# The last 1 MB of an output projection: one row slot sent in 102 + 26 partitions, two more cut by columns, the result stored in three parts

## The chip, the cores and the metric

The kernel runs on one core of a Trainium2 chip. The metric is device time of one execution in microseconds (us): the median of several runs. A profile of one execution gives a span, from the first to the last instruction.

## The reference

Four tokens (B = 4, one position each, D = 1024) pass through a cached attention block and a gated MLP, and the two results are mixed. Cut to what matters:

```
g = sigmoid((x * gate_w).sum(-1))
q = x @ wq                                   # wq: 1024 x 4096, 32 heads of 128
p = softmax(q . k_cache / sqrt(128))         # k_cache, v_cache: 4 x 32 x 8192 x 128, bf16
a = (p . v_cache) @ wo                       # wo: 4096 x 1024
b = x + sigmoid(x.w_r) * ((silu(x @ w_gate) * (x @ w_up)) @ w_down)
out = g * a + (1 - g) * b                    # 4 x 1 x 1024, bf16
```

The caches are 256 MB each, so the program is one long stream of reads from HBM: 576 MB in all, against 8 KB written.

## The kernel before

All large reads go through one SBUF buffer, the `ring`, and are issued by SyncE (SP) in one fixed order. The K pairs and V pairs of the cache come first, alternating; while they stream, VectorE transposes K, TensorE computes scores and the weighted sums, and the gate/up/down weights are read in between. `wo` (8 MB) comes last, as eight blocks `g` of 1 MB. A block holds 512 rows of `wo`: partition `p` gets rows `4p` to `4p+3`, four "row slots" of 1024 columns (2 KB) each (`wov`, `FR = 4`). Blocks 0 and 1, and 2 and 3, come in one transfer each (`wo_two`, L455); blocks 4 to 6 in one transfer each; block 7 is cut: row slots 0 and 1 together (128 partitions x 4 KB), row slot 2 (128 x 2 KB), and row slot 3 in two halves of 512 columns (128 x 1 KB each). These are issued in `wo_block` (L439, L442).

Of each transfer, 16 DMA engines carry a share. SP has eight completion semaphores for its transfers and uses them in turn, so that a transfer is issued only when the one eight places ahead of it has landed.

`wo_block` also returns `use()`, the matmuls of that piece: for each row slot, one matmul of 512 columns into `acc(0)` and one into `acc(1)` (through `mm_acc`, L296), with `LT`, the transposed attention result, as the weights. `acc(0)` and `acc(1)` are two PSUM banks that hold output columns 0 to 511 and 512 to 1023; everything of the output is summed up there. `acc(0)` lies on partitions 0 to 3 and `acc(1)` on 32 to 35, so a pair of matmuls, one into each, runs side by side.

After the last `use()`, VectorE copies `acc(0)` to SBUF as bf16 (L694) and SP stores it (L695); ScalarE copies `acc(1)` (L696) and issues its store itself (L697). SP then waits for the completion of every semaphore, and all engines meet at a barrier (L723).

The order of the engines' instructions is the order in which the program is written (a manual schedule). `keep_weights` drops repeated weight loads, `drop_implied` drops waits that another wait already implies.

Of the kernel before, what the change touches and what calls it, by code (L numbers as in the profile page):

```python
# [112 lines left out]
def kernel(  # L113
# [15 lines left out]
    nc = tc.nc  # L129
    P = 128  # L130
    Bn, Sq, D = A_x.shape
# [17 lines left out]
    FR = 4  # L149
    FG = F // (P * FR)  # L150
    NB = 512
    NH = D // NB
# [7 lines left out]
    out2 = out.rearrange("b s d -> (b s) d")  # L160
# [28 lines left out]
    def turned(rows, n, dtype=BF, lo=0):  # L189
        t = TB[tb_turn[0] % 2]  # L190
        tb_turn[0] += 1
        return t[lo:lo + rows, 0:n] if dtype == BF else t[lo:lo + rows, 0:2 * n].bitcast(dtype)
# [46 lines left out]
    n = 1  # L239
# [19 lines left out]
    for half in range(2):  # L259
        for e in range(2):  # L260
            nc.gpsimd.tensor_copy(out=R[:, 2 * half + e].rearrange("p (n j) -> p n j", n=4),
                                  in_=ident[:, 64 * half + e:64 * half + 64:2].unsqueeze(1).to_broadcast([P, 4, 32]))
# [21 lines left out]
    LT = const.tile([P, FR, H // FR, Bn], BF)  # L284
# [7 lines left out]
    def acc(n):  # L292
        return A_ps[n][32 * n:32 * n + Bn]

    def mm_acc(n, lhsT, rhs, start=False):
        nc.tensor.matmul(acc(n), lhsT=lhsT, rhs=rhs, start=start, stop=True, skip_group_check=True)  # L296
# [36 lines left out]
    wov = A_wo.rearrange("(g p r) n -> p g r n", p=P, r=FR)  # L333
# [86 lines left out]
    NWB = H // WB  # L420
# [8 lines left out]
                                 rhs=OT[:, WB * g0 + k:WB * g1:WB, :], start=True, stop=True, skip_group_check=True)  # L429
        nc.vector.tensor_copy(out=LT[:, :, g0:g1, :], in_=lp)  # L430

    def wo_block(g, r0=0, r1=FR, half=None, load=True):

        at = wo_places[g] * FR * D
        w = flat[:, at:at + FR * D].rearrange("p (r n) -> p r n", r=FR)
        if not load:
            pass
        elif half is None:
            nc.sync.dma_start(out=w[:, r0:r1].rearrange("p r n -> p (r n)"),  # L439
                              in_=wov[:, g, r0:r1].rearrange("p r n -> p (r n)"))  # L440
        else:
            nc.sync.dma_start(out=w[:, r0, half * NB:(half + 1) * NB], in_=wov[:, g, r0, half * NB:(half + 1) * NB])  # L442

        def use():
            for r in range(r0, r1):
                for n in range(NH) if half is None else [half]:
                    mm_acc(n, LT[:, r, g, :], w[:, r, n * NB:(n + 1) * NB])
        return use


    def wo_two(g):

        at = wo_places[g] * FR * D
        assert wo_places[g + 1] == wo_places[g] + 1
        nc.sync.dma_start(out=flat[:, at:at + 2 * FR * D].rearrange("p (g n) -> p g n", g=2),  # L455
                          in_=wov[:, g:g + 2].rearrange("p g r n -> p g (r n)"))
        return [wo_block(g, load=False), wo_block(g + 1, load=False)]
# [14 lines left out]
    def flush_sums():  # L472
        while full:
            full.pop(0)()
# [186 lines left out]
    for kind, d in order:  # L661
# [11 lines left out]
        if (kind, d) == ("v", ND - 1):  # L673
            first, second = wo_two(0)
            first()
            last = [second]
# [2 lines left out]
        if (kind, d) == ("v", ND - 2):  # L679
            o_rows(0, GE)  # L680
    last += wo_two(2)
    cuts = [(g, 0, FR) for g in range(4, NWB - 1)] + [(NWB - 1, 0, 2), (NWB - 1, 2, 3)] + [(NWB - 1, FR - 1, FR, n) for n in range(NH)]
    last += [wo_block(*cut) for cut in cuts]
    flush_sums()
    for _ in range(2):
        last.pop(0)()
# [4 lines left out]
    for use in last:  # L691
        use()
    res = [turned(Bn, NB, lo=32 * n) for n in range(NH)]
    nc.vector.tensor_copy(out=res[0], in_=acc(0))  # L694
    nc.sync.dma_start(out=out2[:, 0:NB], in_=res[0])  # L695
    nc.scalar.copy(out=res[1], in_=acc(1))  # L696
    nc.scalar.dma_start(out=out2[:, NB:D], in_=res[1])  # L697


# [28 lines left out]
```

## Time and profile before

| what | us |
|---|---|
| median of 3 runs | 1341.02 (1340.89 to 1341.03) |
| span of the profiled execution | 1339.17 |
| outside the span, against the median | 1.85 |
| last `wo` transfer landed, from the span's start | 1335.98 |
| last matmul ends | 1336.40 |
| stores landed (SP's, ScalarE's) | 1338.09, 1338.33 |

The page gives the span in 40 slices, the DMA engines' busy share and the bytes per second, the chain of work that ended last, and groups of instructions. The times of landing are records of the trace: each DMA engine that carried a part of a transfer adds one to the transfer's semaphore when its part is written, and each such step has a time. A transfer over all 128 partitions has 16 of them.

### The profile page before, as it was taken

The numbers are of one execution on the slowest core, as the hardware profiler recorded it, in microseconds if no ns is written. First come the engines' busy times: TensorE is split into PE (matmuls) and PEld (weight loads), VectorE is DVE, ScalarE is ACT, GpSimd is POOL, SyncE is SP. The second block draws the span as 40 slices with busy tenths as digits, with TensorE's granted clock in tenths as the row PEclk, the third lists the DMA queues.
The fourth block names the chain that finished last, engine by engine and source line by source line (L and its number), as shares of the span: only waits on it lengthen the run. The fifth ranks groups of instructions, "written<-read, shape, count | busy, mean of one in ns | idle before, by whom it ended". The sixth has DMA issues, their size and how long they took to land.

```text
span 1339.2 us, 6936 instructions
## 1 busy us (share of the span) xinstructions
PE 1031.3 (77%) x4654; PEld 139.8 (10%) x1486; DVE 638.7 (48%) x385; ACT 57.7 (4%) x58; POOL 67.0 (5%) x174
## 2 busy tenths in 40 slices
PE   2386787887777788777787977777797778687887
PEld 0011000001010010101001110100111011111111
DVE  2285998556553436555352556634345556100001
ACT  0000000100010000100010000100000000110000
POOL 2000000100010000100010000100001000100000
PEclk9697998898888998888889988888998889689999
DMA  9999999999999999999999999999999999999998
GB/s 415 433 437 437 435 437 435 420 438 433 433 435 437 427 433 435 429 438 431 433 431 433 435 439 427 429 433 435 438 430 428 433 429 429 438 429 445 422 422 352
DMA packets 13032, 576.14 MB, mean 430 GB/s; under 512 B 1436, under 2 KB 1700, under 8 KB 1970
## 3 DMA queue, kind: packets, MB, share of 16 engines
q1 hardware_dynamic: 12994, 575.69, 99.6%
q8 instruction: 24, 0.39, 0.1%
q14 instruction: 6, 0.05, 0.0%
q10 hardware_dynamic: 8, 0.00, 0.0%
HBM read 575.68 MB, written 0.01 MB: 430 GB/s over the span
## 4 chain that ended last, share of the span: by engine, by line
DMA 67%; PE 22%; DVE 9%; POOL 0%; ACT 0%; issue 0%; SPq 0%
DMA ring<-in_A_k_cache_dram 53%; PE S_ps L516 15%; DMA ring<-in_A_v_cache_dram 10%; DVE ring L511 9%; PE o_ps L587 5%; DMA ring<-in_B_w_gate_dram 3%; DMA ring<-in_A_wo_dram 2%; PE o_ps L342 1%; POOL PB L570 0%; DVE mx L536 0%; PE led L633 0%; ACT TB L545 0%; PE acc L296 0%; POOL Z L492 0%; PE o_ps L633 0%
## 5 line engine op out<-in xcount | busy, mean ns | idle before, releaser
L511 DVE STREAM_TRANSPOSE ring<-ring 128x2048 uint32<-128x2048 uint32 x256 | 566.5, 2276 | 307.7 <-DMA ring<-in_A_k_cache_dram 307.7
L516 PE MATMUL S_ps<-ring,Z 128*128 128x512 bf16 x2048 | 519.9, 408 | 229.3 <-DVE ring L511 216.1
L587 PE MATMUL o_ps<-ring,PB 128*64 128x512 bf16 x2048 | 457.4, 384 | 35.7 <-DMA ring<-in_A_v_cache_dram 33.3
L516 PEld LDWEIGHTS <-Z 128*128 128x128 bf16 x512 | 53.0, 104 | 683.0 <-issue 683.0
L617 DVE SCALAR_TENSOR_TENSOR OS<-o_ps,mE,OS 128x512 f32<-128x512 f32 x33 | 24.8, 751 | 161.7 <-ACT OS L613 160.2
L587 PEld LDWEIGHTS <-PB 128*64 128x64 bf16 x512 | 56.7, 111 | 428.3 <-issue 427.6
L625 DVE SCALAR_TENSOR_TENSOR OS<-o_ps,mE,OS 128x512 f32<-128x512 f32 x5 | 3.7, 750 | 143.6 <-ACT OS L623 143.6
L492 POOL COPY Z<-qa 32x4 bf16<-32x4 bf16 x128 | 25.8, 201 | 716.7 <-PE S_ps L516 689.6
L570 POOL COPY PB<-PT 32x1024 bf16<-32x1024 bf16 (+3 forms) x23 | 33.4, 1452 | 466.6 <-PE o_ps L587 360.7
L613 ACT ACTIVATE OS<-o_ps,mE 128x512 f32<-128x512 f32 x11 | 7.6, 687 | 671.2 <-PE o_ps L587 671.2
L568 ACT COPY PB<-PT 32x1024 bf16<-32x1024 bf16 (+3 forms) x21 | 30.3, 1444 | 22.4 <-PE o_ps L587 17.4
L545 ACT ACTIVATE TB<-S_ps,mx 128x2048 bf16<-128x2048 f32 x4 | 7.9, 1967 | 321.7 <-DVE mx L542 321.7
L254 PE MATMUL S_ps<-identb,x 6*128 6x6 bf16 x8 | 0.6, 196 | 22.3 <-DMA x<-in_gate_w_dram 22.3
L342 PE MATMUL o_ps<-ring,xw 128*4 128x512 bf16 (+2 forms) x128 | 12.9, 490 | 3.5 <-DMA ring<-in_B_w_gate_dram 3.5
L633 PEld LDWEIGHTS o_ps<-selg,OS 128*128 128x128 f32 x88 | 11.5, 191 | 8.8 <-issue 8.5
L550 DVE STREAM_TRANSPOSE PT<-TB 128x2048 bf16<-128x2048 bf16 x4 | 9.2, 2312 | 6.4 <-ACT TB L545 6.4
L296 PE MATMUL acc<-ring,hT 128*4 128x512 bf16 x54 | 7.9, 466 | 5.5 <-DMA ring<-in_B_w_down_dram 5.5
L536 DVE TENSOR_REDUCE mx<-S_ps 128x1 f32<-128x2048 f32 x4 | 9.1, 2282 | 6.0 <-PE S_ps L516 6.0
L296 PE MATMUL acc<-ring,LT 128*4 128x512 bf16 x64 | 8.8, 378 | 3.3 <-DMA ring<-in_A_wo_dram 2.8
L633 PE MATMUL o_ps<-selg,OS 128*128 128x8 f32 x88 | 10.5, 245 | 0.0
L623 ACT ACTIVATE OS<-o_ps,mE 128x512 f32<-128x512 f32 x5 | 3.4, 687 | 151.2 <-PE o_ps L587 151.2
L256 DVE COPY xw<-S_ps 128x48 bf16<-128x48 bf16 x1 | 0.2, 184 | 17.5 <-PE S_ps L254 17.5
(83 smaller groups left out, 88.4 us busy)
## 6 DMA issues: line engine op xcount, KB each, us to landing
ring<-in_A_v_cache_dram SPq DMA_DIRECT2D x7, 4096.0 KB
ring<-in_A_k_cache_dram SPq DMA_DIRECT2D x6, 4096.0 KB, 33.9
ring<-in_A_v_cache_dram SPq DMA_DIRECT2D x6, 2048.0 KB, 28.9
ring<-in_B_w_gate_dram SPq DMA_DIRECT2D x1, 7168.0 KB
ring<-in_B_w_up_dram SPq DMA_DIRECT2D x1, 7168.0 KB
ring<-in_B_w_down_dram SPq DMA_DIRECT2D x1, 6912.0 KB
ring<-in_A_wo_dram SPq DMA_DIRECT2D x2, 2048.0 KB
ring<-in_A_wo_dram SPq DMA_DIRECT2D x3, 1024.0 KB, 34.5
```

What stands on the lines that cost most here:

```text
L296: nc.tensor.matmul(acc(n), lhsT=lhsT, rhs=rhs, start=start, stop=True, skip_group_check=True)
L342: nc.tensor.matmul(ps[32 * k:32 * k + Bn, z, :].rearrange("p (f r) -> p f r", r=FR)[:, :, lo:hi], lhsT=xT[TW * half + t], rhs=rhs, start=( ...
L492: nc.gpsimd.tensor_copy(out=Z[at, :, QP - 1 + QP * q], in_=qa[at, :, h0 + q, b])
L511: nc.vector.transpose(out=kn[:, half], in_=kn[:, half])
L516: nc.tensor.matmul(sps[:, z, :], lhsT=Z[:, 2 * half + e, s:s + P], rhs=T[:, half, 16 * z:16 * z + 16, :, e], start=(t + k + half + e == 0) ...
L536: nc.vector.tensor_reduce(out=mx[:, 0:1], in_=sps[:].rearrange("p z n -> p (z n)"), axis=AX.X, op=ALU.max)
L550: nc.vector.transpose(out=PT[:].rearrange("p j i -> p (j i)"), in_=PTs)
L568: nc.scalar.copy(out=Bv[at, :, :, q, :], in_=Pv[at])
L570: nc.gpsimd.tensor_copy(out=Bv[at, :, :, q, :], in_=Pv[at])
L587: nc.tensor.matmul(o_ps[w // 2][row:row + NM, w % 2, :], lhsT=PB[:, RD * (d % NW) + n, z].rearrange("p w s j -> p (w s j)"), rhs=vn[:, j0 ...
L617: nc.vector.scalar_tensor_tensor(out=OS[:], in0=o_ps[w // 2][:, w % 2, :], scalar=mE[:, w:w + 1], in1=OS[:], op0=ALU.mult, op1=ALU.add)
L633: nc.tensor.matmul(oT, lhsT=OS[:, q * Dh:(q + 1) * Dh], rhs=selg[:, q].rearrange("p t s -> p (t s)"), start=(q == 0), stop=(q == 3), skip_ ...
```

## The change

In the last block, row slots 0 and 1 are no longer one transfer. Row slot 0 is a transfer of its own (128 x 2 KB). Row slot 1 is sent as two transfers, partitions 0 to 101 and 102 to 127. Row slots 2 and 3 are cut by columns: columns 0 to 767 of both slots in one transfer (128 x 2 x 1.5 KB), then columns 768 to 1023 of slot 2 and of slot 3 in one transfer each (128 x 0.5 KB). The bytes are the same; four transfers become six. `use()` follows the cuts: columns 512 to 767 and 768 to 1023 become separate matmuls of 256 columns.

At the end, ScalarE now copies and stores `acc(0)`; VectorE copies `acc(1)` in two parts of 256 columns, and SP stores each part. The other blocks go through the same rewritten `wo_block` with the same transfers as before.

```diff
-    def wo_block(g, r0=0, r1=FR, half=None, load=True):
+    def wo_block(g, r0=0, r1=FR, cols=(0, D), load=True, spans=((0, P),)):
 
         at = wo_places[g] * FR * D
+        c0, c1 = cols
         w = flat[:, at:at + FR * D].rearrange("p (r n) -> p r n", r=FR)
-        if not load:
-            pass
-        elif half is None:
-            nc.sync.dma_start(out=w[:, r0:r1].rearrange("p r n -> p (r n)"),
-                              in_=wov[:, g, r0:r1].rearrange("p r n -> p (r n)"))
-        else:
-            nc.sync.dma_start(out=w[:, r0, half * NB:(half + 1) * NB], in_=wov[:, g, r0, half * NB:(half + 1) * NB])
+        for p0, p1 in spans if load else ():
+            if c1 - c0 == D:
+                nc.sync.dma_start(out=w[p0:p1, r0:r1].rearrange("p r n -> p (r n)"),
+                                  in_=wov[p0:p1, g, r0:r1].rearrange("p r n -> p (r n)"))
+            else:
+                nc.sync.dma_start(out=w[p0:p1, r0:r1, c0:c1], in_=wov[p0:p1, g, r0:r1, c0:c1])
 
         def use():
             for r in range(r0, r1):
-                for n in range(NH) if half is None else [half]:
-                    mm_acc(n, LT[:, r, g, :], w[:, r, n * NB:(n + 1) * NB])
+                for n in range(NH):
+                    lo, hi = max(c0, n * NB), min(c1, (n + 1) * NB)
+                    if lo < hi:
+                        nc.tensor.matmul(acc(n)[:, lo - n * NB:hi - n * NB], lhsT=LT[:, r, g, :], rhs=w[:, r, lo:hi],
+                                         start=False, stop=True, skip_group_check=True)
         return use
...
-    cuts = [(g, 0, FR) for g in range(4, NWB - 1)] + [(NWB - 1, 0, 2), (NWB - 1, 2, 3)] + [(NWB - 1, FR - 1, FR, n) for n in range(NH)]
-    last += [wo_block(*cut) for cut in cuts]
+    LC = D - NB // 2
+    cuts = [(g, 0, FR) for g in range(4, NWB - 1)] + [(NWB - 1, 0, 1), (NWB - 1, 1, 2), (NWB - 1, 2, FR, (0, LC))]
+    cuts += [(NWB - 1, r, r + 1, (LC, D)) for r in range(2, FR)]
+    last += [wo_block(*cut, spans=((0, 102), (102, P)) if cut[1:3] == (1, 2) and cut[0] == NWB - 1 else ((0, P),)) for cut in cuts]
...
     res = [turned(Bn, NB, lo=32 * n) for n in range(NH)]
-    nc.vector.tensor_copy(out=res[0], in_=acc(0))
-    nc.sync.dma_start(out=out2[:, 0:NB], in_=res[0])
-    nc.scalar.copy(out=res[1], in_=acc(1))
-    nc.scalar.dma_start(out=out2[:, NB:D], in_=res[1])
+    nc.scalar.copy(out=res[0], in_=acc(0))
+    nc.scalar.dma_start(out=out2[:, 0:NB], in_=res[0])
+    for lo, hi in ((0, LC - NB), (LC - NB, NB)):
+        nc.vector.tensor_copy(out=res[1][:, lo:hi], in_=acc(1)[:, lo:hi])
+        nc.sync.dma_start(out=out2[:, NB + lo:NB + hi], in_=res[1][:, lo:hi])
```

## The prediction

> **What bounds the kernel now.** First the page: span, bytes per second by slice, and the chain that ended last.
>
> ```profile
> span 1339.2 us, 6936 instructions
> ...
> GB/s 415 433 437 437 435 437 435 420 438 433 433 435 437 427 433 435 429 438 431 433 431 433 435 439 427 429 433 435 438 430 428 433 429 429 438 429 445 422 422 352
> ...
> q8 instruction: 24, 0.39, 0.1%
> ...
> DMA 67%; PE 22%; DVE 9%; POOL 0%; ACT 0%; issue 0%; SPq 0%
> ```
>
> The stream runs at 415 to 445 GB/s until the last slice, 352. The change touches the last megabyte of 576, so all it can reach lies in that slice. Next the chain in order of time and the timeline, both at the end:
>
> ```profile
> 1311.27 24.05 DMA ring<-in_A_wo_dram
> 1335.32 0.04 issue
> 1335.36 1.05 PE acc L296 x4
> 1336.41 0.02 issue
> 1336.43 0.58 ACT TB L696
> ```
>
> ```profile
> 1334.70 1.69 PE L296 MATMUL acc<-ring,LT 128*4 128x512 bf16 x8 [0.22 <-DMA ring<-in_A_wo_dram]
> 1336.12 0.68 DVE L694 CAST TB<-acc 4x512 bf16<-4x512 f32 x1 [6.49 <-PE acc L296]
> 1336.43 0.58 ACT L696 CAST TB<-acc 4x512 bf16<-4x512 f32 x1 [10.90 <-PE acc L296]
> 1336.83 0.29 SPq L695 DMA_DIRECT2D out_dram<-TB  x1
> 1337.04 0.55 ACTq L697 DMA_DIRECT2D out_dram<-TB  x1
> ```
>
> The end hangs on the last `wo` landing, then one matmul, one copy, one store, the barrier. Last, the DMA share in windows (the last two columns are DMA share and GB/s):
>
> ```profile
> 1328.00:1330.00 2.00, 2.00 (x35) 1.09 (x35) 0.43 (x2) 0.00 (x0) 0.00 (x0) 1.00 1.02 422
> 1330.00:1332.00 2.00, 1.22 (x10) 0.35 (x8) 0.00 (x0) 0.00 (x0) 0.00 (x0) 1.00 0.91 362
> 1332.00:1333.00 1.00, 0.02 (x2) 0.00 (x0) 0.00 (x0) 0.00 (x0) 0.00 (x0) 1.00 0.65 264
> 1333.00:1334.00 1.00, 0.54 (x6) 0.26 (x7) 0.00 (x0) 0.00 (x0) 0.00 (x0) 1.00 0.74 276
> 1334.00:1335.00 1.00, 0.78 (x10) 0.25 (x5) 0.00 (x0) 0.00 (x0) 0.00 (x0) 1.00 0.54 201
> ```
>
> From 1330 on the share falls: some DMA engines are out of work while others go on. The landing records of the last `wo` transfer say how many (us after 1331.23, one number per engine):
>
> ```
> 0.00 0.22 0.32 0.69 | 2.97 2.97 3.21 3.53 | 4.34 4.37 4.44 4.48 4.51 4.54 4.66 4.75
> ```
>
> Four engines are early, four in the middle, eight late. Perfect balance would end at the mean, 3.13, a gain of 1.6 us, or 0.12%. About 0.2% (2.7 us) is what a measurement of this kernel can tell from no change, so this step is small by construction.
>
> **Which engine is which.** The landings count the engines a transfer uses: 16 for 128 partitions, 8 for the 8-row transfer of `w_down`, 4 for the 4 rows of `x`, and 3 for its 12-row transfers, whose source is 3 outer by 4 inner rows (four 10 KB packets on each of three engines). All fit the largest number up to 16 that divides the outer counts of both sides. So 102 partitions go to 6 engines, 17 rows each, and 26 to 13 engines, 2 rows each. [...]
>
> [...] Before those transfers seven engines were early (0.00 to 0.62 after 1136.44) and nine were 3.04 or more behind. The three (call them 0 to 2) were among the seven and came out at 3.1 to 3.7: they are three of the four in the middle now (2.97, 3.21, 3.53). [...]
>
> The late ones have a cause: each 16 KB instruction packet (q8, 24 in all) takes one engine for about 1.0 us and leaves it about 1.5 us behind. They go round eight engines in turn; after 24, each of the eight has three. [...]
>
> **Part 1, the DMA end.** Packet rows, net of overlap: 4 KB 155 ns, 2 KB 80, 1 KB 42.4; the line through them (4.7 ns plus 36.7 per KB) gives, as estimates, 61.5 for 1.5 KB and 23.5 for 0.5 KB. A completion packet adds about 6. Row slots 0 to 3 cost each engine before: 8 x 155 + 8 x 80 + 16 x 42.4 + 4 x 6 = 2.58 us. After:
> - engines 0 to 5: (8 + 17 + 2) x 80 + 16 x 61.5 + 16 x 23.5 + 6 x 6 = 3.56, so +0.97;
> - engines 6 to 12: (8 + 2) x 80 and the rest alike = 2.20, so -0.39;
> - engines 13 to 15: 2.02, so -0.56.
>
> The late eight then end at 1335.98 - 0.39 = 1335.59. Engine 2's share ends at 1331.23 + 3.53 + 0.97 = 1335.73, and is the new last: **-0.25**. Bounds: -0.39 if the middle engines gain less, and +0.97 if a late one is among 0 to 5. 0.5 KB packets are smaller than any read in this trace; at the 1 KB price of 42.4 they would add 0.30 to every engine, at half of it nothing.
>
> [...]
>
> **Part 2, issue.** SP issues a transfer when the one eight places ahead has landed. Two more transfers mean that the last two wait for blocks 2-3 (landed 1325.98) and block 4 (1328.46), not for V pieces. SP's store row shows 0.77 us from issue to first packet, so the last piece can move from 1329.25. The earliest engines reach it at about 1330.3. Nothing is queued behind SP's wait but the stores. Cost 0; without the 1 us of cover, early engines would wait that long, and they have 4 us. The extra SP instructions (0.3 to 0.4 each) lie beside the stream.
>
> **Part 3, from the last landing to the store.** Before: matmul 0.04 after landing, 0.376 long, ScalarE copy 0.036 later and 0.577 long, its store issued after 0.03 and landed 1.29 later: 1335.98 to 1338.33, 2.35 in all. After:
> - TensorE still has two pairs (0.215 apart) when the column piece lands, 2 x (8 x 0.0235 + 0.006) = 0.39 before the last: +0.04 (0 to 0.15).
> - The last matmul has 256 columns: half a pair less, 0.27 for 0.376: -0.11.
> - VectorE's two copies. In the compiled order only the first has a wait, and that is for the last matmul, so neither starts early. A 96-column cast took 258 ns and the 512-column one 679, 1.01 ns per column: 0.42 for 256. Two dependent-free copies at L625 started 0.67 apart for 0.75: so 0.42 + 0.34 = 0.76 for 0.577: +0.18 (0.10 to 0.27).
> - The second store, by SP, takes 1.265 (its row: 1336.83 to 1338.09) for 1.29: -0.03; behind the first it may be 0.1 later.
> - ScalarE's copy of `acc(0)` needs the column piece only and starts about 0.1 before the last matmul ends, so its store lands some 0.3 before SP's second. Off the path.
>
> Sum **+0.09** (-0.1 to +0.4).
>
> **Part 4, the exit.** SP passes one wait after the other on all completion semaphores; its records step 0.068 us apart. Before, the waits for the two stores were the last two, and the drain came 0.065 after the last. In the compiled order after, the first wait is for the second SP store, the last to land, and five more follow: 5 x 0.068 = **+0.34** (0 if they pass together).
>
> Sum: -0.25 + 0.09 + 0.34 = +0.18. Span 1339.17 + 0.18 = 1339.35; with 1.85 outside it, 1341.02 + 0.18 = **1341.2**.
>
> **Rivals.**
> - *A late engine is among 0 to 5.* The turn of instruction packets need not follow numbers. [...] Such an engine ends at 1335.57 to 1335.98 plus 0.97: +0.6 to +0.97 instead of -0.25; with +0.43 behind it, +1.0 to +1.4: **1342.2**. It decides as soon as one engine beyond 3.78 in the list above is among the six. [...] Chance 0.25.
> - *The balance pays and the tail is free.* If SP's six waits pass at once and the copies hide, -0.25 to -0.4 is left: **1340.7**. Against it: the 0.068 steps stand in the trace. Chance 0.13.
> - *102 and 26 rows go to fewer engines, slower beyond doubt.* With two engines each, 51 + 13 rows x 80 ns = 5.1 us instead of 0.64 on engines 0 and 1, which have at most 1.8 us of room: +2.9 at the DMA end, with +0.43 **1344.3**; on one engine each, 128 x 80 = 10.2 us, about 1350. It decides below about three engines. Against it: three engines for 12 rows, so that powers of two are not needed. Chance 0.04.
> - *The change doesn't do what it says.* The result leaves in three parts, but by the compiled waits no part of `acc(1)` leaves before the last matmul; that is in the sum already.
>
> **How the numbers follow.** Forecast 0.58, the others 0.25, 0.13, 0.04. The range 1340.6 to 1342.5 takes in the first three with their bounds and leaves out little more than the fourth. Only the fourth passes 2.7 us, so slower 0.05; no case gains as much, faster 0.01; same 0.94.
>
> **What would show it.** Landings of the 102-partition transfer: six engines. Last `wo` landing near 1335.7 in place of 1335.98, with no gap of more than 0.5 us between it and the next engines. Two VectorE copies of about 0.42 us, both behind the last matmul. SP's drain about 0.35 us after the last store landed. A last landing after 1336.3 would show a late engine among the six.

## The result and the profile after

The kernel after takes 1343.65 us (median of 16 runs, 1342.86 to 1344.09); the kernel before took 1341.01 in as many runs beside it (1340.80 to 1342.25). The medians are 2.64 us apart, and 1343.65 lies outside the range 1340.6 to 1342.5. The ratio over all these runs is 1.0017, 95% interval 1.0011 to 1.0024, or some 2.3 us. By the prediction's own measure (0.2%, 2.7 us) the times alone would hardly tell this from no change; but the interval lies above 1, and the two profiles show the loss step by step. The profiled execution took 1343.64 with a span of 1341.86, so 2.69 of span more, and the same 1.8 outside it. Two kernels below each had one execution of over 2400 us, which is left out; with the stores alone it was the profiled one, so that run has times only.

First the page: the span, and the bytes by slice.

```profile
span 1341.9 us, 6944 instructions
...
GB/s 415 440 428 438 434 434 436 425 439 430 436 434 428 434 436 434 430 432 436 430 436 434 430 428 436 432 438 436 438 415 440 430 430 432 436 428 442 426 420 318
```

Only the last slice differs much: 318 GB/s where it was 352. The stream before it is as it was. Next the end of the chain that ended last (start, length, what):

```profile
1320.94 16.58 DMA ring<-in_A_wo_dram
1337.51 0.04 issue
1337.55 1.13 PE acc L449 x4
1338.68 0.02 issue
1338.71 0.42 DVE TB L702
1339.12 0.33 DVEq L729
```

The same order of steps as before, but each starts later: TensorE's last stretch at 1337.55 for 1335.36, the copy at 1338.71 for 1336.43. Most of the loss is there before the first matmul of that stretch. The windows of this end (the last three columns are TensorE's granted clock, DMA share and GB/s):

```profile
1328.00:1330.00 2.00, 2.00 (x33) 0.95 (x34) 0.43 (x2) 0.00 (x0) 0.00 (x0) 1.00 1.04 404
1330.00:1332.00 2.00, 0.94 (x10) 0.34 (x8) 0.00 (x0) 0.00 (x0) 0.00 (x0) 1.00 0.85 289
1332.00:1333.00 1.00, 0.17 (x2) 0.00 (x0) 0.00 (x0) 0.00 (x0) 0.00 (x0) 1.00 0.85 291
1333.00:1334.00 1.00, 0.00 (x0) 0.00 (x0) 0.00 (x0) 0.00 (x0) 0.00 (x0) 0.61 0.71 198
1334.00:1335.00 1.00, 0.77 (x4) 0.22 (x5) 0.00 (x0) 0.00 (x0) 0.00 (x0) 0.50 0.79 230
```

Read the last two columns against each other. From 1330 to 1332 the engines are busy 0.85 of the time and move 289 GB/s, 340 per unit of busy share; before, 0.91 moved 362, or 398. From 1333 to 1334 it is 279 against 373. The engines are not idle for want of work: packets of the same size keep them busy for longer (their durations are shown below). And the clock column falls to 0.50, which no row of before at this place has.

The landing records of the last `wo` transfer (us after 1330.87, one per engine) show both faults of the DMA end:

```
0.00 0.06 0.55 | 2.75 | 5.09 5.32 5.35 5.44 5.44 5.45 5.58 5.61 5.65 5.67 5.98 | 7.04
```

The last engine lands at 1337.91, where before the last landed at 1335.98. It is 1.06 behind the next one; but that next one, at 1336.85, is itself later than the whole stream before. Last, the timeline of the tail:

```profile
1334.23 2.29 PE L449 MATMUL acc<-ring,LT 128*4 128x512 bf16 x10 [2.07 <-DMA ring<-in_A_wo_dram]
...
1336.73 0.59 PE L449 MATMUL acc<-ring,LT 128*4 128x512 bf16 x2 [0.20 <-DMA ring<-in_A_wo_dram]
...
1337.55 1.01 PE L449 MATMUL acc<-ring,LT 128*4 128x512 bf16 x6 [0.24 <-DMA ring<-in_A_wo_dram]
...
1338.60 0.57 ACT L699 CAST TB<-acc 4x512 bf16<-4x512 f32 x1 [13.20 <-PE acc L449]
1338.71 0.75 DVE L702 CAST TB<-acc 4x256 bf16<-4x256 f32 x2 [9.21 <-PE acc L449]
1339.15 0.63 SPq L703 DMA_DIRECT2D out_dram<-TB  x2
```

TensorE waited 2.07 us before 1334.23, and its ten matmuls then take 2.29 us, at a granted clock of 0.50: a pair each 0.43, where at 1.00 it was 0.215. The path from the last landing, step by step (records of both traces, us):

| step on the path | before | after | difference | forecast |
|---|---|---|---|---|
| last `wo` landing | 1335.98 | 1337.91 | +1.93 | -0.25 |
| to the end of the last matmul | 0.42 | 0.66 | +0.24 | -0.07 |
| to the start of the copy | 0.04 | 0.14 | +0.10 | 0 |
| copy or copies | 0.58 | 0.75 | +0.17 | +0.18 |
| to the landing of the last store | 1.32 | 1.24 | -0.08 | -0.03 |
| to SP's drain | 0.08 | 0.40 | +0.32 | +0.34 |
| sum | | | +2.68 | +0.18 |

### The profile page after: what moved, and what is told of

Its sections match the earlier page's. It is cut to its first block, busy times and chain, and to the rows that moved or that the text cites. A ratio compares the mean times of both kernels' runs of the same rounds, so it can differ in the third digit from the quotient of the medians.

```text
span 1341.9 us, 6944 instructions
## 1 busy us (share of the span) xinstructions
PE 1035.9 (77%) x4656; PEld 141.0 (11%) x1488; DVE 638.9 (48%) x386; ACT 57.8 (4%) x58; POOL 67.0 (5%) x174
## 4 chain that ended last, share of the span: by engine, by line
DMA 66%; PE 23%; DVE 9%; POOL 0%; issue 0%; ACT 0%; SPq 0%; DVEq 0%
DMA ring<-in_A_k_cache_dram 52%; PE S_ps L519 16%; DMA ring<-in_A_v_cache_dram 10%; DVE ring L514 9%; PE o_ps L590 7%; DMA ring<-in_B_w_gate_dram 3%; DMA ring<-in_A_wo_dram 1%; PE o_ps L342 1%; POOL PB L573 0%; PE led L636 0%; DVE mx L539 0%; ACT TB L548 0%; PE acc L449 0%; POOL Z L495 0%; PE o_ps L636 0%
## 5 line engine op out<-in xcount | busy, mean ns | idle before, releaser
L449 PE MATMUL acc<-ring,LT 128*4 128x512 bf16 (+1 forms) x66 | 10.1, 430 | 4.4 <-DMA ring<-in_A_wo_dram 4.0
```

The source lines that it names most:

```text
L449: nc.tensor.matmul(acc(n)[:, lo - n * NB:hi - n * NB], lhsT=LT[:, r, g, :], rhs=w[:, r, lo:hi], start=False, stop=True, skip_group_check=True)
```

## The experiments

My theory after the result: the split of row slot 1 is the cause, in two parts, one late engine among the six and a slowing of all packets while the split rows are written. The rivals: the small column pieces, the stores, and TensorE's clock alone.

### One part of the change at a time

**Row slot 1 in one transfer**, everything else as after:

```diff
-    last += [wo_block(*cut, spans=((0, 102), (102, P)) if ...
+    last += [wo_block(*cut, spans=((0, P),) if ...
```

> The changed kernel with one part undone: row slot 1 in one transfer of 128 partitions (five transfers in the last block instead of six); column pieces and stores stay changed. Theory (the 102-partition transfer is the cause, by its load on six engines and by slowing every engine's packets while it runs): packets go back to 309, 84, 65 and 27 ns for 8, 2, 1.5 and 0.5 KB; each engine carries 16 x 80 + 16 x 61 + 16 x 23 + 5 x 6 = 2.65 us of the last block against 2.58 before, so the last wo landing is at 1336.05; the clock stays at 1.0; with a tail 0.4 longer than before (two VectorE copies, six waits at the exit) the span is 1339.6 to 1339.8 and the time 1341.4 to 1341.6. Rival (the column pieces of 1.5 and 0.5 KB rows slow the stream): packets stay 1.2 to 1.4 times as long, the last landing is past 1336.8 and the time above 1342.4.

Measured: 1341.63 (1341.30 to 1342.15; before, beside it, 1341.12), ratio 1.0004 [0.9994, 1.0013]. Two of the 2.6 us are gone, and packets take what they took before (2 KB 1.00 to 1.04 of the minimum). From 1330 to 1332 the engines are busy 0.96 of the time and move 379 GB/s, 395 per unit of busy share, against 398 before and 340 after. The last landing is at 1336.28, 0.23 later than the theory had it.

**The split alone**, in the kernel before (row slots 2 and 3 and the stores as there):

```diff
-    cuts = [(g, 0, FR) for g in range(4, NWB - 1)] + [(NWB - 1, 0, 2), (NWB - 1, 2, 3)] + [(NWB - 1, FR - 1, FR, n) for n in range(NH)]
-    last += [wo_block(*cut) for cut in cuts]
+    cuts = [(g, 0, FR) for g in range(4, NWB - 1)] + [(NWB - 1, 0, 1), (NWB - 1, 1, 2), (NWB - 1, 2, 3)]
+    cuts += [(NWB - 1, 3, FR, (n * NB, (n + 1) * NB)) for n in range(NH)]
+    last += [wo_block(*cut, spans=((0, 102), (102, P)) if cut[1:3] == (1, 2) and cut[0] == NWB - 1 else ((0, P),)) for cut in cuts]
```

> The kernel before with the split of row slot 1 alone (slot 0, then 102 and 26 partitions, slot 2 whole, slot 3 in two halves of 512 columns, stores as before). Theory (the split is the cause): 8 KB packets of other engines at 330 to 390 ns while the 102 partitions are under way, one engine about 1 us behind the others, last landing 1337.4 to 1338.0, tail as before or 0.2 longer if the clock falls, span 1340.6 to 1341.4, time 1342.4 to 1343.3. Rival (column pieces): packets as before, span below 1339.9, time below 1341.8.

Measured: 1343.26 (1342.84 to 1343.43; before 1341.12), ratio 1.0013 [1.0004, 1.0022]. The last landing is at 1337.67, one engine 1.03 behind the next. The split costs 2.1 us by itself; it needs neither the columns nor the stores.

**The stores alone**, in the kernel before:

```diff
-    nc.vector.tensor_copy(out=res[0], in_=acc(0))
-    nc.sync.dma_start(out=out2[:, 0:NB], in_=res[0])
-    nc.scalar.copy(out=res[1], in_=acc(1))
-    nc.scalar.dma_start(out=out2[:, NB:D], in_=res[1])
+    nc.scalar.copy(out=res[0], in_=acc(0))
+    nc.scalar.dma_start(out=out2[:, 0:NB], in_=res[0])
+    for lo, hi in ((0, NB // 2), (NB // 2, NB)):
+        nc.vector.tensor_copy(out=res[1][:, lo:hi], in_=acc(1)[:, lo:hi])
+        nc.sync.dma_start(out=out2[:, NB + lo:NB + hi], in_=res[1][:, lo:hi])
```

> The kernel before with the stores alone changed (ScalarE for acc(0), VectorE for acc(1) in two parts of 256 columns, SP stores each part). My sum of the tail: last landing as before at 1335.98; last matmul still 512 columns; two copies 0.75 for 0.58, store 0.08 shorter, six waits one after the other 0.31 longer: plus 0.35 to 0.5, span 1339.5 to 1339.7, time 1341.4 to 1341.5. Rival (the stores' new order costs nothing or the exit waits pass together): span 1339.1 to 1339.3, time 1341.0 to 1341.1.

Measured: 1341.29 (1341.11 to 1341.90) against 1341.12, ratio 1.0000 [0.9990, 1.0009]. That lies between the two expectations, and the interval does not part them. The exit and copy rows of the table above are the better evidence for what the stores cost.

**The columns alone** (whole row slot 1, stores of before):

```diff
-    last += [wo_block(*cut, spans=((0, 102), (102, P)) if ...
+    last += [wo_block(*cut, spans=((0, P),) if ...
...
-    nc.scalar.copy(out=res[0], in_=acc(0))
...
+    nc.vector.tensor_copy(out=res[0], in_=acc(0))
...
```

> The kernel after with row slot 1 in one 128-partition transfer and with the stores of the kernel before: of the change only the column cut (768, 256) is left. Theory A (the split cost 2.2 us, the stores 0.2 to 0.4, the columns next to nothing): 1341.0 to 1341.2, within 0.15 us of the kernel before; last landing 1336.0 to 1336.15, the last matmul about 0.1 us shorter, the exit as before. Theory B (the small pieces cost something of their own, by smaller packets or by one more transfer in SP's queue): 1341.3 to 1341.6, as much as the kernel with whole row slot 1 and three stores, with the last landing past 1336.2. Theory C (the shorter last matmul and the shorter last piece gain): 1340.7 to 1340.9.

Measured: 1341.48 (1341.19 to 1342.11; before 1341.06), ratio 1.0004 [0.9995, 1.0013]; the median fits the second theory (1341.3 to 1341.6), the last landing, 1336.13, the first, and the interval does not settle it. The timeline shows a place that none of the three theories named:

```profile
1336.45 0.68 DVE L699 CAST TB<-acc 4x512 bf16<-4x512 f32 x1 [6.79 <-PE acc L449]
1336.56 0.58 ACT L701 CAST TB<-acc 4x512 bf16<-4x512 f32 x1 [10.99 <-PE acc L449]
1337.16 0.29 SPq L700 DMA_DIRECT2D out_dram<-TB  x1
1337.16 0.54 ACTq L702 DMA_DIRECT2D out_dram<-TB  x1
```

Before, VectorE's copy ran at 1336.12, ahead of ScalarE's at 1336.43, because the half of row slot 3 for `acc(0)` had landed first (1335.66; the other half 1335.98). With the columns cut at 768, `acc(0)` is completed only just before `acc(1)`: both copies run together, and both stores are issued at 1337.16. ScalarE's store lands 1.55 us after its issue instead of 1.29. Landing +0.15, matmul -0.11, copy start +0.08, store +0.26 and SP's waits +0.11 make 0.49, against a span that is 0.5 longer.

### What the split does

**An even split, 96 + 32.** By the landing counts 96 and 32 partitions each go to all 16 engines, 6 and 2 rows each, so every engine carries 8 rows as in one transfer, and only the cut by partitions is left:

```diff
-    ... spans=((0, 102), (102, P)) ...
+    ... spans=((0, 96), (96, P)) ...
```

> [...] Theory A (packets are slow because engines write partitions that belong to others' share): packets of 2 and 8 KB are still 1.1 to 1.4 times as long while slot 1 is under way, and the last landing is at 1336.4 to 1336.9, span 1340.2 to 1340.9. Theory B (only the uneven load of six engines matters): as with slot 1 whole, last landing 1336.05 to 1336.15, span 1339.6 to 1339.9.

Measured: 1342.58 (1342.02 to 1343.34; before 1341.12), ratio 1.0009 [1.0000, 1.0019]. No engine is far behind the others, yet 8 KB packets take up to 1.43 times their minimum (mean of a half microsecond) and the last landing is at 1336.95, a little past what theory A allowed. So the load is not all of it: where the load is equal, the landing is still 0.67 us later than with row slot 1 whole. The medians differ by 0.95, for TensorE's clock falls here too, to 0.50 from 1333.09 on: from the last landing to the end of the last matmul it takes 0.80 us, against 0.33 with row slot 1 whole.

**Five engines (85 + 32 + 11 partitions) and four (68 + 60).** The same line with other cuts. If the late engine of the six is number 5, taking it out must take away the last lagging landing.

> The changed kernel with slot 1 cut into 85, 32 and 11 partitions: five engines carry 17 rows (0 to 4), the others 2 or 3. If engine 5 is the late one among the six of the changed kernel, its lag of 1.06 us goes and the last landing falls from 1337.9 to about 1336.9, time 1342.4 to 1342.8. If the late one is engine 3 or 4, the lag stays, time 1343.4 to 1343.9.

> The changed kernel with slot 1 cut into 68 and 60 partitions: engines 0 to 3 carry 17 and 4 rows, eleven others 4, one none. If the late engine is number 4 or 5, no engine lags by about 1 us any more: last landing 1336.6 to 1337.0, time 1342.3 to 1342.8. If it is engine 3, it has two rows more than in the changed kernel and lags by 1.0 to 1.2 us: time 1343.5 to 1344.0. In both cases packets are slow while the 68 and 60 partitions are under way.

Measured: 1342.29 (1341.91 to 1342.91) and 1342.38 (1341.96 to 1342.81), ratios 1.0008 [0.9998, 1.0017] and 1.0008 [0.9999, 1.0018]. The three engines that land last do so within 0.08 us of each other with five (to 1336.72) and within 0.18 with four (to 1336.65). With six, one was 1.06 behind. So neither the five nor the four hold a late one. No trace names the engine of a landing; if the five are among the six, as the author took them to be, the late one is the sixth, called number 5 here. Packets are still slow (2 KB up to 1.6 times with five), though no late engine gets more rows: with five engines the last landing is 0.44 us later than with row slot 1 whole. The landings also count 5, 16 and 11 engines, and 4 and 15, as the prediction's rule for the number of engines has it.

**The same rows, written to other partitions.** Two kernels that differ in one number. The 102 rows go out in the same shares, 17 packets of 2 KB on each of six engines, but not to their places: the 17 rows of share `e` (0 to 5) go into a single partition in another part of the ring, partition `4e` in the one, `64 + 4e` in the other. Both leave these rows out of the sum.

```diff
-            if c1 - c0 == D:
+            if (p0, p1) == (0, 102):
+                nc.sync.dma_start(out=flat[0:0+24:4, 5 * UN:5 * UN + 17 * D].rearrange("p (b n) -> p b n", b=17),
+                                  in_=wov[0:102, g, r0].rearrange("(a b) n -> a b n", b=17))
+            elif c1 - c0 == D:
```

The other has `flat[64:64+24:4, ...` in the same line.

> [...] Theory (packets are slow because engines write into partitions that other engines also write): 2 and 8 KB packets go back to 84 and 309 ns, only the engine that is late remains behind, by 1.0 us; last landing 1336.5 to 1337.0, time 1342.0 to 1342.6. Rival (the slow part is on the reading side, 17 consecutive rows per engine, or lies in the uneven load): packets stay 1.2 to 1.4 times as long, time 1343.2 to 1343.8.

> As the run with six partitions 0 to 20, but into partitions 64, 68, 72, 76, 80 and 84; the same rows, packets and engines, and the same part of the sum left out. [...] Rival (reading side or uneven load): the same as with partitions 0 to 20, within 0.3 us.

Measured: 1342.22 (1342.01 to 1342.60), ratio 1.0006 [0.9997, 1.0016], and 1344.79 (1344.03 to 1345.13), ratio 1.0026 [1.0016, 1.0035]. The same packets from the same rows on the same engines, 2.57 us apart, 2.26 of it at the last landing (1336.89 and 1339.15). Here is the DMA view of 1326 to 1339 in 40 slices, first partitions `4e`, then `64 + 4e`:

```profile
DMA  9999999999999999789757877874100000000000
GB/s 403 429 403 429 429 403 403 403 375 402 402 397 416 402 392 384 301 332 364 314 208 269 292 274 269 299 249 129 46 24 22 17 0 0 0 0 0 0 0 19
```

```profile
DMA  9999999999999989787988777988678876641100
GB/s 429 454 429 479 403 403 429 454 410 388 397 399 389 358 307 340 290 315 271 247 176 222 183 148 148 178 148 159 148 188 192 176 142 148 178 120 61 39 16 0
```

In the 21st to the 26th slice the engines are 5 to 8 tenths busy in the first kernel and 7 to 9 in the second, yet the first moves 208 to 299 GB/s and the second 148 to 222. Its last landing comes seven slices (0.325 us each) later. Packet durations say the same (mean of a half microsecond, as a multiple of the shortest):

```
2 KB packets from    1330.5  1331.0  1331.5  1332.0  1332.5  1333.0  1333.5  1334.0  1334.5
before                 1.03       -       -    1.00    1.00    1.00    1.00    1.00    1.00
after                  1.41    1.22    1.07    1.01    1.29    1.41    1.29    1.17    1.50
partitions 4e          1.02    1.01    1.00    1.00    1.00    1.00    1.00    1.00    1.00
partitions 64 + 4e     2.17    1.47    1.24    1.22    2.00    1.55    1.97    1.94    2.06
```

With partitions `4e` the 2 KB packets are as quick as before (8 KB ones within 4%), and only the late engine is left: its last landing is at 1336.89, again 1.06 behind the next. With `64 + 4e` the 2 KB packets take 1.22 to 2.17 times their shortest, and the 8 KB packets of the transfers ahead grow longer as well: 1.44 and 1.71 times in the two half microseconds from 1332.0, against 1.01 and 1.00 with `4e`. So the partitions written set the price. That other engines write `64 + 4e` in the transfers around them is the author's guess: no trace shows which engine writes which partition.

### TensorE's clock

Eight matmuls of 512 columns, into a PSUM bank that is free by then, ahead of block 6's:

```diff
+    def fill():
+        for i in range(8):
+            nc.tensor.matmul(o_ps[0][0:Bn, 0, :], lhsT=LT[:, 0, 0, :], rhs=flat[:, 0:NB], start=True, stop=True, ...)
+    last.insert(len(last) - 6, fill)
```

> The kernel after with eight matmuls of 512 columns added ahead of block 6's, into a PSUM bank that is no longer needed; the output does not use them. They fill most of the 2.07 us in which TensorE waited before 1334.23. Theory A (the half clock after 1333.2 follows from that wait, and costs the end 0.24 us): the granted clock stays near 1.0 up to the last matmul, a pair of matmuls steps by 0.215 us again and not 0.42, the time from the last landing to the end of the last matmul goes from 0.66 to about 0.42, and the median falls by 0.2 to 0.35 us, to 1343.3 to 1343.45. Theory B (the clock falls for another reason, or the matmuls were not on the path): the clock still falls to 0.5 near 1333 to 1335, or the landing is as late and the end does not move: 1343.6 to 1343.75. In both the last landing stays near 1337.9, one engine about 1 us behind the rest.

Measured: 1343.31 (1343.16 to 1343.65), ratio to before 1.0016 [1.0006, 1.0025]; 0.34 below after, which did not run beside it (before 1341.06 here, 1341.01 there). The times alone could not show a difference of this size; the timeline does:

```profile
1334.27 1.24 PE L449 MATMUL acc<-ring,LT 128*4 128x512 bf16 x10 [0.27 <-DMA ring<-in_A_wo_dram]
...
1337.55 0.67 PE L449 MATMUL acc<-ring,LT 128*4 128x512 bf16 x6 [0.44 <-DMA ring<-in_A_wo_dram]
...
1338.28 0.75 DVE L707 CAST TB<-acc 4x256 bf16<-4x256 f32 x2 [8.77 <-PE acc L449]
```

The ten matmuls take 1.24 instead of 2.29, the clock stays at 1.00 up to 1340.66, and the copies start at 1338.28 instead of 1338.71. The last landing is at 1337.91 as in the kernel after. From there to the end of the last matmul it takes 0.31 instead of 0.66. So the half clock cost about 0.35 us, as the first theory had it, and a little more than its 0.24. The matmuls added do work that nothing needs; they mend a fault that the change brought, for before the clock held to the last matmul (1.00 in the step to 1336.46; it ends at 1336.40).

No part of the change, alone or with another, came out below the kernel before (1341.29, 1341.48, 1341.63 and 1343.26, against 1341.06 and 1341.12).

## Why the prediction was wrong, point by point

- **How many engines: right.** The 102-partition transfer has six landings, the 26-partition one 13.
- **Part 1, the DMA end: wrong, by 2.18 us, and this is the step that failed.** It put -0.25 where +1.93 was measured. Two things in it failed.
  - *No late engine among the six.* The sum puts +0.97 on engines 0 to 5 and has the late eight outside them. No run shows which engines a transfer to six takes, or that none of them is late; what the runs showed in its place is one landing 1.06 behind the next with six engines, and the last three within 0.08 and 0.18 of each other with five and four. The numbers came from the author's guess that the instruction packets go round by engine number, from 6 on. The rival had this case at the right price: +0.6 to +0.97 at the DMA end, and 1342.2 in all. The kernel with partitions `4e` has this fault without the slow packets, and gives +0.91 and 1342.22; that the median agrees to 0.02 is chance.
  - *One price for a packet, wherever it is written.* No rival had this. The 61.5 and 23.5 ns for 1.5 and 0.5 KB were good (65 and 27 are the shortest in the trace, some 4 of it overlap; the slope beside them should read 37.7 per KB, not 36.7), but steadily so only from 1336 on. Between 1329 and 1335.5 most half microseconds show 1.1 to 1.5 times the shortest duration. The two kernels above show that the partitions written bear on this (2 KB packets at 1.00 to 1.02 times their shortest into 0 to 20, at 1.22 to 2.17 into 64 to 84); that the 102 and 26 rows go mostly to partitions that another engine writes in the transfers around them was the author's guess, and no run shows it. Every row that the price was taken from came from 128-partition transfers. Against the kernel with partitions `4e`, this cost 1.02 us at the landing.
  - Whole row slot 1 lands at 1336.28, +0.30; the late engine adds 0.61, the slow packets 1.02: together the +1.93. The shares hold for this order only. With five engines, where no late one gets more rows, the slow packets alone put the landing 0.44 past whole row slot 1; that kernel is still 0.74 later than before, so the right guess on the late engines would not have made -0.25. Of the +0.30, half may be scatter: the columns alone, with the same transfers, landed at 1336.13.
- **Part 1, the split as such.** The prediction had it gain from the uneven landings. With row slot 1 in one transfer the kernel is 2.0 us quicker than with the two (1341.63, 1343.65).
- **Part 2, issue: right.** No gap at a queue stands on the path.
- **Part 3, from landing to store: right but for the clock.** The two copies took 0.75 (forecast 0.76), the store -0.08 (forecast -0.03). At full clock (1.00, with the eight added matmuls) the time from landing to the end of the last matmul fell by 0.11, to 0.31 (forecast -0.07); at half clock (0.50, the kernel after) it rose by 0.24, to 0.66. The forecast had taken the clock of before for granted. Missing was also 0.10 for VectorE's later start behind the last matmul.
- **Part 4, exit: right.** SP's six waits begin at 1340.710, .769, .841, .905, .967 and 1341.026, and the drain at 1341.094: +0.32 for +0.34.
- **What would show it.** The last landing is after 1336.3, as written for a late engine; but the 96 + 32 split lands at 1336.95 without one, so it is the gap of 1.06 to the next landing that tells. The rest of the lateness shows only in packet durations, or in GB/s per busy share, which the list did not ask for.

## What to carry to other kernels

Count bytes and rows per engine, but also ask where the rows are written: here the 2 KB rows of the transfer cut by partitions, and those that ran beside them, took up to 1.5 times as long, and the same rows on as many engines took 1.00 to 1.02 times their shortest into partitions 0 to 20 and up to 2.17 times into 64 to 84. To even out the load of the engines, an estimate from uneven landings needs the number of every engine that gets more work: one late engine among the six set the end, 1.06 us behind the next, whatever room the other five had. Around a tail, look at what cuts do to the order of endings: columns cut at 768 let two stores, that had left one after the other (1336.83 and 1337.04), leave together (both 1337.16).

## What the runs showed of the hardware

**Other partitions, another time.** 102 rows on six engines into partitions 64 to 84 instead of 0 to 20: 1344.79 against 1342.22 us, 2 KB packets up to 2.17 times their shortest against 1.02. Why, no run shows; it is not the six engines alone, for 8 KB packets of the transfers ahead took up to 1.71 times as long too.

**The clock's records come in steps of 3.413 us.** In eleven traces the records of the granted clock at the end (but for the last, which the end cuts) are 3.413 us long or a multiple of that (64.853 = 19 steps, 68.267 = 20, 71.680 = 21, 78.507 = 23). In these traces, whether it falls goes with how busy TensorE was in the step before. The windows view cut at these steps, for the kernel after, for the 96 + 32 split and for the kernel before (length, then PE busy; the third column from the right is the clock):

```profile
1329.80:1333.22 3.42, 1.30 (x12) 0.34 (x8) 0.00 (x0) 0.00 (x0) 0.00 (x0) 1.00 0.85 288
1333.22:1336.63 3.41, 2.29 (x10) 0.48 (x9) 0.00 (x0) 0.00 (x0) 0.00 (x0) 0.50 0.63 185
```

```profile
1329.68:1333.09 3.41, 1.54 (x14) 0.44 (x10) 0.00 (x0) 0.00 (x0) 0.00 (x0) 1.00 0.90 321
1333.09:1336.51 3.42, 2.33 (x12) 0.75 (x12) 0.00 (x0) 0.00 (x0) 0.00 (x0) 0.50 0.58 188
```

```profile
1329.64:1333.05 3.41, 1.60 (x14) 0.50 (x11) 0.00 (x0) 0.00 (x0) 0.00 (x0) 1.00 0.84 336
1333.05:1336.46 3.41, 2.66 (x16) 0.68 (x15) 0.34 (x1) 0.03 (x1) 0.00 (x0) 1.00 0.40 150
```

Among the last five steps of each of the eleven traces, at full clock, every one with 1.54 us of work or less is followed by half clock (those over 1 us: 1.03, 1.03, 1.07, 1.30, 1.36, 1.43, 1.54), and none with 1.60 or more (the least: 1.60, 1.65, 1.68, 1.79, 1.80). At half clock 2.29 and 2.33 did not bring full clock back, 3.17 and 3.39 did. That is no sharp limit: over the whole of these traces, all 356 full-clock steps with under 1.35 us are followed by half clock and 2955 of the 2970 with 1.60 or more are not, but of the 46 between them 32 kept full clock and 14 lost it. At half clock, none of the 469 steps with under 2.60 us brought full clock back, and 374 of the 382 above did. The eight added matmuls made the step from 1330.42 on 2.58 us busy, and the clock held at 1.00.
